# Seven Strassen products for the gate and up projections of an adaLN block

## The chip, the cores and the metric

The kernel runs on one core of a Trainium2 chip. Its engines are PE (TensorE, matmuls into PSUM), PEld (TensorE's weight loads, which overlap with PE), DVE (VectorE), ACT (ScalarE), POOL (GpSimd) and SP (SyncE, which issues the DMAs here). The metric is the device time of one execution in microseconds.

## The reference

One transformer block with adaptive layer norm on 2048 tokens of width 576: attention over the last 512 cached keys, then a gated feed-forward layer with 4608 hidden units. Everything is float32. Cut to what matters:

```python
h = _layernorm(x, axis=-1) * (1 + ca) + sa
x = x + ga * _A_ref(h, A_k_cache, A_v_cache, A_wq, A_wo)   # 32 heads of 128, 512 keys each
h = _layernorm(x, axis=-1) * (1 + cb) + sb
g = h @ w_gate                 # (2048, 576) x (576, 4608)
u = h @ w_up
x = x + gb * ((_sigmoid(g) * u) @ w_down)
```

The six rows sa, ca, ga, sb, cb, gb come from silu(c) @ w_mod.

## The kernel before, in words

Every matmul runs in `float32r`. To keep float32's accuracy, each operand is split into a high part (ACT copies it to `float32r`) and a low part (DVE or POOL subtracts the high part), and a product is three matmuls: high x low, low x high, high x high (`three`, `pairs_a`). The width 576 is four chunks of 128 and a tail of 64; the tail's high and low parts are laid on top of each other in 128 rows, so that it takes two matmuls. One product of 128 hidden units with a block of 512 tokens is so 14 matmuls of 512 columns.

Tokens are in four blocks of 512 (`blk`). Attention runs in two halves of two blocks each, 32 heads, written as a list of steps (`at_step`, `at_n`) in which weights, keys, norms and transposes of later steps are given a place by hand; a scheduler then fixes the order on each engine. The norms of the feed-forward layer for blocks 0 and 1 are at the end of this list (`norm_block(..., True, ...)`: DVE, POOL, five PE transposes per 128 tokens, ACT and DVE to write the two parts `hTm` and `hTt`). Blocks 2 and 3 follow in the first steps of the feed-forward loop.

The feed-forward loop goes over slices of 128 hidden units (`f`, 36 of them), and for each over the four blocks: 144 steps. A step computes gate and up for one block (L613: 28 matmuls of 512 columns into the banks `st` and `ot`), takes the sigmoid on ACT (L617), multiplies on DVE (L618), splits the result into `hs` (ACT L620, POOL L621), and beside it does the down products of the step two before: 8 tiles of three matmuls of 288 columns (L238, called from `down_mm`), each added into the residual `x` by DVE (L602). The weights of slice f+1 are loaded by SP (`load_a` L196 and L198, `load_b` L221) and split (ACT L203, POOL L204 and L205 for gate and up; POOL L225, ACT L227, POOL L229 for down) during slice f; each slice is loaded once for all four blocks. The pool of raw weights has four buffers, that of split weights four and two.

Around the loop, the last attention steps and the first feed-forward steps overlap, since the pools are shared and the first two slices are loaded from the attention's list of steps.

Of the kernel before, what the change touches and what calls it, by code (L numbers as in the profile page):

```python
# [16 lines left out]
P = 128  # L17
# [7 lines left out]
def adaln_block_kernel(ctx: ExitStack, tc: tile.TileContext, x, k_cache, v_cache, wq, wo, w_gate, w_up, w_down,  # L25
# [23 lines left out]
    wp = ctx.enter_context(tc.tile_pool(name="wp", bufs=1))  # L49
    ps = ctx.enter_context(tc.tile_pool(name="ps", bufs=1, space=bass.MemoryType.PSUM))  # L50
# [10 lines left out]
    def ps_qp():  # L61
        return psum("qp", 1, [P, BLK])
# [35 lines left out]
    ones = const.tile([P, P], F32, name="ones")  # L98
# [5 lines left out]
    def mod_rows(tag):  # L104
        return const.tile([P, D], F32, tag=tag, name=tag)
# [38 lines left out]
    def ln_stats(b, t):  # L144
        if t == 0:
            LN[b] = [wp.tile([P, TPB, 2], F32, tag="mv", name="mv", bufs=2),
                     wp.tile([P, TPB], F32, tag="ln_y", name="ln_y", bufs=2)]
        mv = LN[b][0]
        st = wp.tile([P, 2, 6], F32, tag="st", name="st", bufs=2)
        for j in range(2):  # L150
            nc.vector.bn_stats(st[:, j, :], xs[b][:, t, j * D2 : (j + 1) * D2])  # L151
        nc.vector.bn_aggr(mv[:, t, :], st)

    def ln_rsqrt(b):
        mv, y = LN[b]
        v = wp.tile([P, TPB], F32, tag="ln_v", name="ln_v", bufs=2)
        a = wp.tile([P, TPB], F32, tag="ln_a", name="ln_a", bufs=2)
# [88 lines left out]
    hTs = {}  # L246
    at = ctx.enter_context(tc.tile_pool(name="at", bufs=1))

    def new_hT(b, late):
        if late and b >= HB:  # L250
            main = at.tile([P, 2 * NC, BLK], F32R, tag="ptt", name="hTm2", bufs=2)
            tail = at.tile([P, 2, BLK], F32R, tag="vs", name="hTt2", bufs=2)
        else:
            main = wp.tile([P, 2 * NC, BLK], F32R, tag="hTm", name="hTm", bufs=2)
            tail = wp.tile([P, 2, BLK], F32R, tag="hTt", name="hTt", bufs=2)
        hTs[b] = (main, tail)

    load_x(0)
    scale, shift, gate = mod_rows("scale"), mod_rows("shift"), mod_rows("gate")
# [19 lines left out]
    new_hT(0, False)  # L279
# [9 lines left out]
    # order of the steps: both token blocks of a head in turn; at the ends of a half, where norms have to be  # L289
    # fitted in, both heads of a block in turn  # L290
# [111 lines left out]
    FA, FB, GA, GB = {}, {}, {}, {}  # L402
# [8 lines left out]
    # weights, keys and values that later steps need  # L411
# [23 lines left out]

    def load_f(f):
        FA[f] = [load_a(w_gate, f * P), load_a(w_up, f * P)]

    def split_f(f):
        GA[f] = [split_a(r) for r in FA.pop(f)]  # L440

    def load_d(f):
        FB[f] = load_b(w_down, f * P)

    def split_d(f):
        GB[f] = split_b(FB.pop(f), rows2["gate"])
# [47 lines left out]
    def norm_block(b, n_stats, n_apply, n_t, step, late, sc_, sh_, mul, add):  # L494
        for t in range(TPB):
            at_n(n_stats + t, ln_stats, b, t)
            at_n(n_apply + t * step, apply_late if late else ln_apply, b, t, sc_, sh_, mul, add)
            at_n(n_t + t * step, ln_transpose, b, t)
        at_n(n_stats + TPB, ln_rsqrt, b)
        at_n(n_t - 1, new_hT, b, late)  # L500

    def apply_late(b, t, scale_, shift_, *eng):
        ln_apply(b, t, rows2["scale"], rows2["shift"], *eng)

    n1 = N // 2
    norm_block(1, -12, -3, -2, 1, False, scale, shift, nc.vector, nc.vector)
    norm_block(2, n1 - 35, n1 - 20, n1 - 14, 2, False, scale, shift, nc.gpsimd, nc.gpsimd)
    norm_block(3, n1 - 30, n1 - 8, n1 - 6, 2, False, scale, shift, nc.gpsimd, nc.gpsimd)

    def mod_make2(key, m, j, add):  # L510
        if j == 0:
            rows2[key] = mod_rows(key + "2")
        mod_make(rows2[key], m, j, add)
# [7 lines left out]
    norm_block(0, N - 40, N - 20, N - 14, 2, True, None, None, nc.gpsimd, nc.gpsimd)  # L521
    norm_block(1, N - 35, N - 8, N - 6, 2, True, None, None, nc.gpsimd, nc.gpsimd)
    at_n(N - 13, load_f, 0)
    at_n(N - 8, split_f, 0)
    at_n(N - 5, load_f, 1)
    at_n(N - 6, load_d, 0)
    at_n(N - 3, split_f, 1)
    at_n(N, split_d, 0)
    at_n(N, load_d, 1)
    at_n(N + 4, split_d, 1)  # L530

# [20 lines left out]
    HS = {}  # L552
    LAG = 2
    order = [(f, b) for bs in ((0, 1), (2, 3)) for f in range(2) for b in bs]
    order += [(f, b) for f in range(2, NF) for b in range(NB)]
    M = len(order)
    turn = [0]

    def down_bank():
        turn[0] += 1  # L560
        return ps_qp()[:, :D2] if turn[0] % 3 == 0 else ps_wo()

    for b in range(HB, NB):
        new_hT(b, True)

    for m in range(0, M + LAG):
        if m < M:
            f, blk = order[m]
            if f > 0 and f + 1 < NF:
                if blk == 0 and f > 1 or f == 1 and blk == 2:  # L570
                    load_f(f + 1)
                if blk == 2 and f > 1 or f == 1 and blk == 3:
                    split_f(f + 1)
                    load_d(f + 1)
                if blk == 3:
                    split_d(f + 1)
        for b, m_stats, m_apply, m_t in ((2, 1, 2, 3), (3, 3, 3, 4)):
            for t in range(TPB):
                if m == m_stats:
                    ln_stats(b, t)  # L580
            if m == m_stats:
                ln_rsqrt(b)
            for t in range(TPB):
                if m == m_apply:
                    ln_apply(b, t, rows2["scale"], rows2["shift"], nc.vector, nc.gpsimd)
                if m == m_t:
                    ln_transpose(b, t)
        todo = []
        if 0 <= m - LAG < M:
            fd, bd = order[m - LAG]  # L590
            todo = [(fd, bd, t, j) for t in range(TPB) for j in range(2)]

        def down_some(k):
            for _ in range(k):
                if not todo:
                    return
                fd, bd, t, j = todo.pop(0)
                hs = HS[fd, bd]
                cols = slice(t * P, (t + 1) * P)
                p = down_mm(hs[:, 0, cols], hs[:, 1, cols], GB[fd], j, down_bank())  # L600
                xv = xs[bd][:, t, j * D2 : (j + 1) * D2]
                nc.vector.tensor_add(xv, p, xv)  # L602
                if fd == NF - 1 and j == 1:
                    nc.sync.dma_start(of[bd][:, t, :], xs[bd][:, t, :])

        if m < M:
            pg, pu = ps_sc(), ps_ot()
            gh = at.tile([P, 2, BLK], F32, tag="kt", name="gh", bufs=2)
            sg, hf = gh[:, 0, :], gh[:, 1, :]
            for p, sp in ((pg, GA[f][0]), (pu, GA[f][1])):  # L610
                pairs = pairs_a(sp, hTs[blk])
                for n, (l, r) in enumerate(pairs):
                    nc.tensor.matmul(p, l, r, start=n == 0, stop=n == len(pairs) - 1)  # L613
                    if n % 4 == 2:
                        down_some(1)
                if p is pg:
                    nc.scalar.activation(sg, pg, AF.Sigmoid)  # L617
            nc.vector.tensor_mul(hf, pu, sg)  # L618
            hs = at.tile([P, 2, BLK], F32R, tag="qt" if m % 2 else "ov", name="hs", bufs=2)
            nc.scalar.activation(hs[:, 0, :], hf, AF.Copy)  # L620
            nc.gpsimd.tensor_sub(hs[:, 1, :], hf, f32(hs[:, 0, :]))  # L621
            HS[f, blk] = hs
        down_some(len(todo))


# [26 lines left out]
```

## Time and profile before

| | |
|---|---|
| median of 3 runs | 3247.59 us (3245.72 to 3248.06) |
| profiled execution: span | 3245.9 us |
| PE busy in the span | 3209.9 us (99%) |
| DVE, ACT, POOL busy | 63%, 37%, 26% |
| granted TensorE clock, mean | 0.998 |
| HBM read, written | 103.52 MB, 4.72 MB |
| first feed-forward matmul, last matmul's end | 1837.6 us, 3241.2 us |

The page gives busy times over the whole span, then 40 equal slices, then the chain of work that ended last. PE is busy in all but the first slices; the ratio of DVE and ACT changes at about 1840 us, where attention ends and feed-forward begins. A busy PE is not PE at its peak, as matmuls are pipelined; how fast they follow each other is read from a timeline.

### The profile page before, as it was taken

What the parts mean: (1) busy time and instruction counts of PE and PEld (TensorE: products, weight loads), DVE (VectorE), ACT (ScalarE), POOL (GpSimd) and SP (SyncE); (2) the same over time, 40 slices, a digit from 0 to 9 for tenths busy, and PEclk for the clock granted to TensorE, in tenths of its full rate; (3) what the DMA queues carried; (4) which work ended last, traced back from release to release, by engine and by line L of the source; (5) the groups of instructions that cost most, each with busy time, mean ns of one, the idle gap of its engine ahead of it and who ended that gap; (6) DMA issues with size and microseconds to landing.
All of it is one profiled execution on the core that took longest, in us unless ns stands there. A gap on an engine that the chain in (4) does not pass through costs nothing.

```text
span 3245.9 us, 45972 instructions
## 1 busy us (share of the span) xinstructions
PE 3209.9 (99%) x17848; PEld 2782.2 (86%) x17848; DVE 2059.6 (63%) x4092; ACT 1211.2 (37%) x2520; POOL 837.2 (26%) x726
## 2 busy tenths in 40 slices
PE   7999999999999999999999999999999999999999
PEld 6888888888888888888888888888888888888888
DVE  8777777777797777777777954444444444444444
ACT  5555555555554555555555421111111111111111
POOL 3322212111132212112121332333322222233321
PEclk9999999999999999999999999999999999999999
DMA  5111111111011111111010000011100000001101
GB/s 176 34 41 45 45 33 35 33 30 37 27 30 33 34 33 34 33 30 37 27 37 27 24 21 24 24 28 28 28 24 25 24 24 24 24 24 28 29 15 59
DMA packets 126747, 111.22 MB, mean 34 GB/s; under 512 B 10432, under 2 KB 101568, under 8 KB 126016
## 3 DMA queue, kind: packets, MB, share of 16 engines
q1 hardware_dynamic: 126528, 108.27, 11.4%
q8 instruction: 141, 2.31, 0.3%
q14 instruction: 78, 0.64, 0.1%
HBM read 103.52 MB, written 4.72 MB: 33 GB/s over the span
## 4 chain that ended last, share of the span: by engine, by line
PE 93%; DVE 3%; DMA 1%; ACT 1%; issue 1%; POOL 0%; SPq 0%; ACTq 0%; POOLq 0%
PE wo L238 21%; PE qp L238 16%; PE st L613 14%; PE ot L613 14%; PE ot L238 10%; PE st L238 10%; PE st L368 7%; DMA raw<-in_A_wq_dram 1%; DVE h L170 1%; PE st L316 0%; ACT pp L357 0%; DVE st L151 0%; DVE x L395 0%; PE st L185 0%; POOL wb L229 0%
## 5 line engine op out<-in xcount | busy, mean ns | idle before, releaser
L602 DVE TENSOR_TENSOR x<-wo,x 128x288 f32<-128x288 f32 x768 | 344.8, 455 | 481.9 <-PE wo L238 481.7
L238 PE MATMUL wo<-wb,ov 128*128 128x288 f32 x3072 | 615.4, 308 | 1.1 <-DVE ov L386 1.1
L371 ACT ACTIVATE ptt<-st 128x512 fp32r<-128x512 f32 x512 | 305.6, 597 | 654.1 <-PE st L368 654.1
L395 DVE SCALAR_TENSOR_TENSOR x<-wo,rs,x 128x288 f32<-128x288 f32 x1024 | 513.1, 512 | 49.9 <-PE wo L238 0.8
L238 PEld LDWEIGHTS wo<-wb,ov 128*128 128x128 f32 x3072 | 482.2, 189 | 49.2 <-DVE ov L386 1.6
L355 DVE TENSOR_REDUCE neg<-st 128x1 f32<-128x512 f32 x512 | 352.0, 687 | 255.2 <-PE st L238 252.7
L613 PE MATMUL st<-hTm,wa 128*128 128x512 f32 x1728 | 493.7, 394 | 0.0
L613 PE MATMUL ot<-hTm,wa 128*128 128x512 f32 x1728 | 489.8, 392 | 0.0
L238 PE MATMUL qp<-hTm,wa 128*128 128x512 f32 x1536 | 444.2, 398 | 3.2 <-DVE hTm L189 1.8
L238 PE MATMUL ot<-ptt,vs 128*128 128x512 f32 x1536 | 442.7, 396 | 0.0
L238 PE MATMUL st<-kt,qt 128*128 128x512 f32 x1536 | 438.1, 393 | 0.1
L238 PEld LDWEIGHTS wo<-wb,hs 128*128 128x128 f32 x2304 | 380.5, 188 | 57.9 <-DVE x L602 3.2
L238 PE MATMUL wo<-wb,hs 128*128 128x288 f32 x2304 | 421.5, 295 | 2.1 <-DVE x L602 2.1
L621 POOL TENSOR_TENSOR hs<-gh,hs 128x512 fp32r<-128x512 f32 x144 | 186.7, 1296 | 749.4 <-ACT hs L620 746.8
L357 ACT ACTIVATE pp<-st,neg 128x512 f32<-128x512 f32 x512 | 350.5, 685 | 60.1 <-DVE neg L355 53.7
L372 DVE TENSOR_TENSOR ptt<-st,ptt 128x512 fp32r<-128x512 f32 x512 | 348.4, 680 | 33.2 <-ACT ptt L371 33.1
L613 PEld LDWEIGHTS ot<-hTm,wa 128*128 128x128 f32 x1728 | 308.7, 188 | 43.8
L204 POOL TENSOR_TENSOR wa<-raw,wa 128x512 fp32r<-128x512 f32 x136 | 176.7, 1299 | 647.1 <-ACT wa L203 572.2
L238 PEld LDWEIGHTS st<-kt,qt 128*128 128x128 f32 x1536 | 288.1, 188 | 62.6 <-DVE hTm L189 0.3
L613 PEld LDWEIGHTS st<-hTm,wa 128*128 128x128 f32 x1728 | 300.2, 187 | 33.3
L602 DVE TENSOR_TENSOR x<-qp,x 128x288 f32<-128x288 f32 x384 | 174.6, 455 | 239.8 <-PE qp L238 239.7
L368 PEld LDWEIGHTS st<-ident,pp 128*128 128x128 f32 x2048 | 253.2, 140 | 83.0 <-ACT pp L357 15.6
(86 smaller groups left out, 3416.8 us busy)
## 6 DMA issues: line engine op xcount, KB each, us to landing
raw<-in_A_wo_dram SPq DMA_DIRECT2D x64, 288.0 KB, 3.0
raw<-in_A_wq_dram SPq DMA_DIRECT2D x64, 256.0 KB, 3.0
raw<-in_B_w_down_dram SPq DMA_DIRECT2D x36, 288.0 KB, 2.8
raw<-in_B_w_gate_dram SPq DMA_DIRECT2D x36, 256.0 KB, 3.0
raw<-in_B_w_up_dram SPq DMA_DIRECT2D x36, 256.0 KB, 2.9
raw<-in_A_k_cache_dram SPq DMA_DIRECT2D x32, 256.0 KB, 2.7
raw<-in_A_v_cache_dram SPq DMA_DIRECT2D x32, 256.0 KB, 2.6
x<-in_A_x_dram SPq DMA_DIRECT2D x4, 1152.0 KB, 7.2
```

The source lines that it names most:

```text
L170: nc.vector.tensor_scalar(h, xs[b][:, t, :], mv[:, t, 0:1], y[:, t : t + 1], op0=OP.subtract, op1=OP.mult)
L204: nc.gpsimd.tensor_sub(sp[:, NC + 1 :, :], raw[:, :NC, :], f32(sp[:, :NC, :]))
L238: nc.tensor.matmul(p, l, r, start=first and n == 0, stop=last and n == len(pairs) - 1)
L355: nc.vector.tensor_reduce(NEG[b][:, i : i + 1], p, axis=AX.X, op=OP.max, negate=True)
L357: nc.scalar.activation(PP[n], p, AF.Exp, bias=NEG[b][:, i : i + 1], accum_out=SUM[b][:, i : i + 1])
L368: nc.tensor.transpose(p[:, k * P : (k + 1) * P], PP[n][:, k * P : (k + 1) * P], ident)
L371: nc.scalar.activation(PT[b][:, 0, :, cols], pv_, AF.Copy)
L372: nc.vector.tensor_sub(PT[b][:, 1, :, cols], pv_, f32(PT[b][:, 0, :, cols]))
L395: nc.vector.scalar_tensor_tensor(xv, p, RS[b][:, i : i + 1], xv, op0=OP.mult, op1=OP.add)
L602: nc.vector.tensor_add(xv, p, xv)
L613: nc.tensor.matmul(p, l, r, start=n == 0, stop=n == len(pairs) - 1)
L621: nc.gpsimd.tensor_sub(hs[:, 1, :], hf, f32(hs[:, 0, :]))
```

## The change

Gate and up of two token blocks are computed together. With the contraction of 576 cut into halves of 288, they are a product of two 2 x 2 matrices of blocks: A11 and A12 are the halves of a slice of `w_gate`, A21 and A22 those of `w_up`; B11 and B21 are the halves of the first block's normed tokens, B12 and B22 those of the second's. Strassen's scheme (in Winograd's form) makes the four results of seven products instead of eight, with sums of weights S1 to S4 and of tokens T1 to T4. A half is two chunks of 128 and a tail of 32; the tail is copied into four strips of 32 rows, which hold high or low parts so that one matmul covers all of the tail's part products. One product is seven matmuls of 512 columns.

- The blocks are taken as pairs (0, 1) and (2, 3), one after the other: 2 x 36 turns (`u`), each with seven products and 48 down matmuls. Each slice's weights are therefore loaded twice.
- The token operands, B11, B21, T1, T2, B22, T3, T4, are computed on DVE and POOL (`pair_norm`, `pair_sums`) and written to two tiles in DRAM, `scr`. For the first pair this is put into the second half of attention, for the second pair into turns 4 to 7. They are read back in two staging buffers (`stage`), transposed on PE and split (`load_combo`) before turn 0, and for the second pair in turn 35.
- The feed-forward has pools of its own, opened after attention's are closed, with `reuse_waits="tile"`. `rw` holds the raw weights of a turn and S1 to S4, with one buffer; `sw` the split ones, with two; `rd` the raw down weights, with one.
- Partial results are kept in SBUF by ACT (`keep`) or accumulated in the same PSUM bank (`a`, `b`, `c`), and added by DVE.

The core of the diff (line numbers of the new loop's functions run from 574 to 774):

```diff
+    def load_w(u):
+        f0 = (u % NF) * P
+        raw = fp.tile([P, 8, 3, P], F32, tag="rw", name="rw", bufs=1)
+        for w, parts in ((w_gate, (A11, A12)), (w_up, (A21, A22))):
+            for half, c in enumerate(parts):
+                r0 = half * D2
+                nc.sync.dma_start(raw[:, c, 0:2, :], w[r0 : r0 + 2 * P, f0 : f0 + P].rearrange("(s p) n -> p s n", p=P))
+                for q in range(4):
+                    nc.sync.dma_start(raw[q * TQ : (q + 1) * TQ, c, 2, :], w[r0 + 2 * P : r0 + D2, f0 : f0 + P])
+        RW[u] = raw
+
+    def sum_w(u):
+        r = RW[u]
+        nc.gpsimd.tensor_add(r[:, S1], r[:, A21], r[:, A22])
+        nc.gpsimd.tensor_sub(r[:, S2], r[:, S1], r[:, A11])
+        nc.gpsimd.tensor_sub(r[:, S3], r[:, A11], r[:, A21])
+        nc.gpsimd.tensor_sub(r[:, S4], r[:, A12], r[:, S2])
+
+    def split_w(u, a):
+        if u not in SW:
+            SW[u] = fp.tile([P, 7, 5, P], F32R, tag="sw", name="sw", bufs=2)
+        r, sw = RW[u][:, a], SW[u][:, a]
+        nc.scalar.activation(sw[:, 0:3, :], r, AF.Copy)
+        nc.vector.tensor_sub(sw[:, 3:5, :], r[:, 0:2, :], f32(sw[:, 0:2, :]))
+        up_ = slice(P // 2, P)
+        nc.gpsimd.tensor_sub(sw[up_, 2, :], r[up_, 2, :], f32(sw[up_, 2, :]))
...
+    def load_combo(pair, c):
+        t = STG.pop((pair, c))
+        ends = fp.tile([P, TPB, 4, TQ], F32, tag="ends", name="ends", bufs=1)
+        nc.scalar.activation(ends, t[:, :, None, 2 * P :].to_broadcast([P, TPB, 4, TQ]), AF.Copy)
+        hc = fp.tile([P, 5, BLK], F32R, tag="hc", name="hc", bufs=7)
+        HC[c] = hc
+        for s in range(3):
+            p = fpsum("w", 4, [P, BLK])
...
+            nc.scalar.activation(hc[:, s, :], p, AF.Copy)
+            if s < 2:
+                nc.vector.tensor_sub(hc[:, 3 + s, :], p, f32(hc[:, s, :]))
+            else:
+                for q in (1, 3):
+                    r = slice(q * TQ, (q + 1) * TQ)
+                    nc.vector.tensor_sub(hc[r, 2, :], p[r], f32(hc[r, 2, :]))
...
+    def product(u, a, c, p, first, downs=(2, 5)):
+        pairs = prod_pairs(u, a, c)
+        for n, (l, r) in enumerate(pairs):
+            nc.tensor.matmul(p, l, r, start=first and n == 0, stop=n == len(pairs) - 1, skip_group_check=not first)
+            if n in downs:
+                down_some(1)
+        if u + 1 < U:
+            split_w(u + 1, a)
...
+    for u in range(U + 1):
...
+        split_d(u)
+        if u + 1 < U:
+            sum_w(u + 1)
+            load_d(u + 1)
...
+        product(u, A11, B11, pa, True)
+        g0 = keep(pa, "g0")
+        product(u, A12, B21, pb, True)
+        nc.vector.tensor_add(g0, pb, g0)
+        nc.scalar.activation(g0, g0, AF.Sigmoid)
+        product(u, S1, T1, pc, True)
+        v1 = keep(pc, "v1")
+        product(u, S2, T2, pa, False)
+        g1 = keep(pa, "g1")
+        product(u, S4, B22, pc, False)
+        nc.vector.tensor_add(g1, pc, g1)
+        nc.scalar.activation(g1, g1, AF.Sigmoid)
+        product(u, S3, T3, pa, False, (2,))
+        nc.vector.tensor_add(v1, pa, v1)
+        nc.vector.tensor_mul(v1, v1, g1)
+        make_hs(u, 1, v1)
+        down_some(5)
+        product(u, A22, T4, pa, False, ())
+        nc.vector.tensor_mul(g0, pa, g0)
+        make_hs(u, 0, g0)
+        down_some(len(todo))
+        if u + 2 < U:
+            load_w(u + 2)
```

Left out above are the calls that stage and load the second pair's operands between the products of turn 35, and those of the second pair's norms (`late_tile`). `load_d` and `split_d` are as before but with one raw buffer; `make_hs` is ACT's copy and POOL's subtraction, as L620 and L621 were.

More of the change, by code (lines that the diff above doesn't have):

```diff
@@ L246, in adaln_block_kernel, with new_hT @@
     hTs = {}
[L247 to L255, printed above, removed]
+    at = actx.enter_context(tc.tile_pool(name="at", bufs=1))
+    def new_hT(b):
+        main = wp.tile([P, 2 * NC, BLK], F32R, tag="hTm", name="hTm", bufs=2)
+        tail = wp.tile([P, 2, BLK], F32R, tag="hTt", name="hTt", bufs=2)
         hTs[b] = (main, tail)
     load_x(0)
-    scale, shift, gate = mod_rows("scale"), mod_rows("shift"), mod_rows("gate")
+    scale, shift, gate = mod_rows("scale", wp), mod_rows("shift", wp), mod_rows("gate", wp)
     wm = {}
@@ new lines, in adaln_block_kernel, with pair_norm @@
+    norm_block(3, n1 - 30, n1 - 8, n1 - 6, 2, scale, shift, nc.gpsimd, nc.gpsimd)
+    scr = [dram.tile([7, P, TPB, D2], F32, tag=f"scr{i}", name=f"scr{i}") for i in range(2)]
+    def pair_norm(pair, t, h, eng):
+        for i in range(2):
+            b = 2 * pair + i
+            mv, y = LN[b]
+            nc.vector.tensor_scalar(h[i], xs[b][:, t, :], mv[:, t, 0:1], y[:, t : t + 1],
+                                    op0=OP.subtract, op1=OP.mult)
+            eng.tensor_mul(h[i], h[i], rows2["scale"])
+            eng.tensor_add(h[i], h[i], rows2["shift"])
@@ L549, in adaln_block_kernel @@
     assert not at_step
[L552 to L622, printed above, removed]
@@ new lines, in adaln_block_kernel, with fpsum, stage @@
+    actx.close()
+    fp = ctx.enter_context(tc.tile_pool(name="fp", bufs=1, reuse_waits="tile"))
+    fps = ctx.enter_context(tc.tile_pool(name="fps", bufs=1, space=bass.MemoryType.PSUM, reuse_waits="tile"))
+    def fpsum(tag, bufs, shape):
+        return fps.tile(shape, F32, tag=tag, name=tag, bufs=bufs)
+    TQ = P // 4
+    B11, B21, T1, T2, B22, T3, T4 = range(7)
+    A11, A12, A22, S1, S2, S3, S4, A21 = range(8)
+    HC, RW, SW, RD, SD, HS = {}, {}, {}, {}, {}, {}
+    STG = {}
+    def stage(pair, c):
+        t = fp.tile([P, TPB, D2], F32, tag="ts", name="ts", bufs=2)
+        nc.sync.dma_start(t, scr[pair][c])
+        STG[pair, c] = t
@@ new lines, in load_d, with split_d @@
+    def load_d(u):
+        f0 = (u % NF) * P
+        raw = fp.tile([P, D], F32, tag="rd", name="rd", bufs=1)
+        nc.sync.dma_start(raw, w_down[f0 : f0 + P, :])
+        RD[u] = raw
+    def split_d(u):
+        raw = RD.pop(u)
+        nc.gpsimd.tensor_mul(raw, raw, rows2["gate"])
+        sp = fp.tile([P, 2, D], F32R, tag="sd", name="sd", bufs=2)
+        nc.scalar.activation(sp[:, 0, :], raw, AF.Copy)
+        nc.gpsimd.tensor_sub(sp[:, 1, :], raw, f32(sp[:, 0, :]))
+        SD[u] = sp
```

168 lines of the change are left out of this document (129 added, 39 removed).

## The prediction

> **What bounds the kernel now.** I read the page from the top: busy times, then the chain of work that ended last. The share of PE (TensorE) in both is the first thing to see, since PE at 99% with a chain that is 93% PE leaves no other engine to relieve.
>
> ```profile
> span 3245.9 us, 45972 instructions
> PE 3209.9 (99%) x17848; PEld 2782.2 (86%) x17848; DVE 2059.6 (63%) x4092; ACT 1211.2 (37%) x2520; POOL 837.2 (26%) x726
> ...
> PE 93%; DVE 3%; DMA 1%; ACT 1%; issue 1%; POOL 0%; SPq 0%; ACTq 0%; POOLq 0%
> ```
>
> Shares over the span mix attention and feed-forward, so I asked for a stretch that holds feed-forward alone, and for the chain in order of time there. The stretch shows PE never idle at a granted clock of 1.00, DVE at 43%, POOL (GpSimd) at 30%. The chain rows give the pace: one gate/up/down step of one block each 3225.87 - 3216.24 = 9.63 us.
>
> ```profile
> 2100.00:3000.00 900.00, 900.00 (x4859) 787.79 (x4858) 388.54 (x840) 161.29 (x258) 267.92 (x233) 1.00 0.09 26
> ...
> 3216.24 0.93 PE st L613 x4
> 3225.87 0.93 PE st L613 x4
> ```
>
> What one matmul costs in a stream is not its duration, since matmuls overlap; the timeline of PE gives it from start to start.
>
> ```profile
> 2508.95 1.09 PE L613 MATMUL ot<-hTm,wa 128*128 128x512 f32 x4
> ...
> 2510.27 0.39 PE L613 MATMUL ot<-hTm,wa 128*128 128x512 f32 x1
> ...
> 2510.96 0.96 PE L238 MATMUL wo<-wb,hs 128*128 128x288 f32 x6
> ...
> L238 PE MATMUL wo<-wb,hs 128*128 128x288 f32 x2304 | 421.5, 295 | 2.1 <-DVE x L602 2.1
> L602 DVE TENSOR_TENSOR x<-wo,x 128x288 f32<-128x288 f32 x768 | 344.8, 455 | 481.9 <-PE wo L238 481.7
> ```
>
> (1.09 - 0.39) / 3 = 0.233 us for 512 columns, (0.96 - 0.30) / 5 = 0.132 us for 288. A step has 28 of the first and 24 of the second: 9.69 us, 0.6% over the 9.63 seen. So the step is its matmuls and nothing else.
>
> **Matmuls removed.** Two steps (two blocks, one slice of 128 hidden units) become one turn of the new loop: seven products of seven matmuls, 49 instead of 56, and the same 48 down matmuls. 49 x 0.233 + 48 x 0.132 = 17.75, scaled by 9.63/9.69 to 17.65 us, against 19.27. Over 72 turns that is 116 us off PE. ACT has under 9 us of work in a turn and DVE about 13 (16 x 0.455, five adds and products at 0.69, seven subtractions of 256 columns at 0.33), by the rows further down; if only work counted, PE would still set the pace.
>
> **The weight tile: a circle of waits.** The raw weights and their four sums lie in one tile, `rw`, with one buffer. In the built program the first load for turn u+2 waits until ACT, DVE and POOL have all finished splitting the seven combinations of turn u+1. Then twenty DMAs follow each other on SP's queue (four of 128 partitions, sixteen of 32; the old loop issues six for the four steps of a slice). Only after the twentieth can POOL add S1, then S2, then S4. The last split stands behind these on POOL, and the next load behind that. Nothing in the circle overlaps with itself, so its length is the pace of the loop if it is above 17.65 us.
>
> SP's part, from its timeline (64-partition strips are the nearest to the 32-partition ones) and from the DMA issues of the page:
>
> ```profile
> 10.82 1.19 SPq L198 DMA_DIRECT2D raw<-in_A_wq_dram  x2
> ...
> 2423.27 0.37 SPq L196 DMA_DIRECT2D raw<-in_B_w_up_dram  x1
> 2423.69 1.15 SPq L198 DMA_DIRECT2D raw<-in_B_w_up_dram  x2
> ...
> raw<-in_B_w_gate_dram SPq DMA_DIRECT2D x36, 256.0 KB, 3.0
> raw<-in_B_w_gate_dram SPq DMA_DIRECT2D x72, 32.0 KB, 2.6
> ```
>
> A wide issue takes 0.42 us to the next start, a strip 1.15 / 2 = 0.575. The last of the twenty starts 4 x 0.42 + 15 x 0.575 = 10.3 us after the first and lands 2.6 later: 12.9 us. Low end: every issue at 0.375, 9.7 us, but S3 and one `hs` subtraction stand ahead of S1 on POOL, so 10.3. High end: a 32-partition strip may cost more than a 64-partition one by as much as that costs more than a wide one (0.2 us): 16.
>
> POOL's part, from the costliest groups, with the timeline for the gap between two of its instructions and for the hop from another engine:
>
> ```profile
> L204 POOL TENSOR_TENSOR wa<-raw,wa 128x512 fp32r<-128x512 f32 x136 | 176.7, 1299 | 647.1 <-ACT wa L203 572.2 <-issue 74.9
> L229 POOL TENSOR_TENSOR wb<-raw,wb 128x576 fp32r<-128x576 f32 x100 | 143.2, 1432 | 652.5 <-ACT wb L227 652.4
> L205 POOL TENSOR_TENSOR wa<-raw,wa 64x128 fp32r<-64x128 f32 x136 | 62.7, 461 | 10.6
> L126 POOL TENSOR_TENSOR wm<-wm 128x288 f32<-128x288 f32 x24 | 19.5, 811 | 41.2 <-ACT wm L123 30.4 <-PE st L368 9.7 <-POOL wa L205 0.3
> ...
> 2498.48 1.29 POOL L204 TENSOR_TENSOR wa<-raw,wa 128x512 fp32r<-128x512 f32 x1 [2.40 <-ACT wa L203]
> 2499.85 0.46 POOL L205 TENSOR_TENSOR wa<-raw,wa 64x128 fp32r<-64x128 f32 x1
> ...
> 2501.52 0.74 ACT L203 ACTIVATE wa<-raw 128x640 fp32r<-128x640 f32 x1 [3.12 <-PE ot L613]
> 2502.39 1.30 POOL L204 TENSOR_TENSOR wa<-raw,wa 128x512 fp32r<-128x512 f32 x1 [2.08 <-issue]
> ```
>
> Sums are 384 wide: between 811 and 1299 ns by width, 1.02 us. In nearly all turns the program's order on POOL from S1 to the next load is S1, down-weight low part, S2, S4, two strips, `hs` low part, three strips, gate product, two strips: 3 x 1.02 + 2 x 1.43 + 1.30 + 7 x 0.46 = 10.45 us, and 13 gaps of 0.08: 11.5. Three hops at 2502.39 - 2502.26 = 0.13 add 0.4. Circle: 12.9 + 11.5 + 0.4 = 24.8 us.
>
> **DVE and POOL get in each other's way.** Seven of DVE's new subtractions per turn read two tiles of SBUF (weights and their high part). The old feed-forward loop has none of these in steady state, only such as read one tile in PSUM. Where they occur, beside POOL, at the start of feed-forward:
>
> ```profile
> L171 DVE TENSOR_TENSOR h<-h,scale x16: 739/746/1600, 15.0 to 1879.4; 128x576 f32<-128x576 f32 x16
> ...
> 1877.05 3.36 POOL L172 TENSOR_TENSOR h<-h,shift 128x576 f32<-128x576 f32 x2 [1.15 <-DVE h L171]
> 1881.20 1.43 POOL L172 TENSOR_TENSOR h<-h,shift 128x576 f32<-128x576 f32 x1 [0.79 <-DVE h L171]
> ...
> 1879.43 1.60 DVE L171 TENSOR_TENSOR h<-h,scale 128x576 f32<-128x576 f32 x1
> ```
>
> The instruction that takes 746 ns took 1600 beside POOL, and POOL's two took 3.36 where two alone take 2.94: POOL lost 0.42. Five of the seven fall inside POOL's part; each is 746 x 256 / 576 = 0.33 us. Between nothing and 5 x 0.33 = 1.65 I take half, 0.8, as the 0.42 is about half of the 0.75: the turn becomes 25.6 us. The Trainium skill (SBUF — State Buffer, "Who interferes with whom") states that a VectorE instruction with two SBUF inputs and a GpSimd one that reads SBUF take turns on a shared port, the second to issue blocked in full. The trace agrees for DVE's 1600 ns; by that rule POOL could lose all 1.65 us, and the turn would be 26.4 us, the kernel 55 us longer than my sum.
>
> PE's 17.65 us lie inside this: its turn waits at S2, whose bank is freed by an ACT copy that stands behind the split of S4, and it idles some 8 us there.
>
> **Edits that cost nothing.** Norms and sums of the first pair move into attention's second half: 4 x (4 x 1.43 + 4 x 0.81) = 36 us of POOL, which is mostly idle there (digits 12 to 22 of its 40 slices below), and eight DVE products, at most 8 x 1.6 = 13 us if that cover were gone. The stores of `scr` have their readers hundreds of us later.
>
> ```profile
> POOL 3322212111132212112121332333322222233321
> ```
>
> **Start, swap, end.** When does attention end without feed-forward products and late norms among it? The first row below is a stretch with L613's matmuls alone, the others are timeline, stretch and groups.
>
> ```profile
> 1836.00:1846.00 10.00, 5.45 (x18) 3.10 (x19) 1.00 0.10 30
> ...
> 1845.08 0.56 PE L238 MATMUL wo<-wb,ov 128*128 128x288 f32 x3
> ...
> 1846.00:1905.00 59.00, 53.64 (x289) 44.72 (x288) 49.03 (x108) 15.06 (x37) 23.23 (x17) 1.00 0.03 9
> ...
> L185 PE MATMUL st<-ident,h 128*128 128x128 f32 x128 | 19.6, 279 | 9.7 <-DVE h L172 9.1 <-DVE hTm L189 0.6
> L186 PE MATMUL wo<-ident,hd 128*128 128x128 f32 x32 | 9.5, 297 | 1.4 <-ACT hd L179 1.4
> ...
> 3240.65 0.56 PE L238 MATMUL qp<-wb,hs 128*128 128x288 f32 x3
> ```
>
> 1845.6 less 18 feed-forward matmuls (4.2) and the transposes of eight token tiles (at most a quarter of 19.6 and of 9.5): 1835. From there to the start of the fourth load I take 70 us, an estimate: the first load is hidden behind attention, the second waits for DVE's statistics of blocks 2 and 3 (14), then come a short turn (19) and one (37) with staging transfers of `hc` among its loads and the second pair's sums on POOL. Bounds: 45 if only two short turns show, 95 if three full turns and a swap's ACT work do. The swap at u = 35 puts 7 x (0.64 + 3 x 0.60) = 17 us on ACT and as much on DVE; some 15 us longer, but the program's order in the five turns after it puts strips ahead of S1, 3 to 4 us shorter each: 0, give or take 15. After the last load 25.6 us to its last split, then PE's rest of turn 70 from S2 on (6), turn 71 (17.65), 48 matmuls (6.3) and the 5 us that follow the last matmul now (3240.65 + 0.56 to 3245.9): 61 in all.
>
> ```profile
> L617 ACT ACTIVATE gh<-st 128x512 f32<-128x512 f32 x144 | 86.0, 597 | 526.4 <-PE st L613 526.4
> L618 DVE TENSOR_TENSOR gh<-ot,gh 128x512 f32<-128x512 f32 x144 | 99.6, 692 | 42.2 <-PE ot L613 40.9 <-PE wo L238 0.6 <-PE qp L238 0.6
> L620 ACT ACTIVATE hs<-gh 128x512 fp32r<-128x512 f32 x144 | 91.8, 638 | 508.0 <-DVE gh L618 506.1
> ```
>
> Sum: 1835 + 70 + 68 x 25.6 (fourth load to last) + 61 = 3707 us of span. The profiled span of 3245.9 lies 1.7 under the median of the three runs, 3247.59, so **3709 us**, 14% slower.
>
> **Rivals.** *PE sets the pace after all.* If the loads and sums of a turn were done by the time PE wants them, the change pays: 3247.6 - 116, plus some 39 for a first turn in which PE has no down matmuls and waits for seven staged operands (50 us against its 11), plus 15 for the swap, less the 5 us that PE idles now from 1846 to 1905: 3181. It decides below a circle of 17.65 us, 8 less than mine; all twenty issues at 0.375, no lock and no gaps still leave over 21. Speaks for it: two thirds of my circle are bounded by rows of other shapes. Chance 0.04.
> *Cheap issues.* Strips issue like wide loads and the lock is free: 10.3 + 11.5 + 0.4 = 22.2 us, 68 x 3.4 less: 3478. The wide issue's 0.37 speaks for it, the strips' 0.575 against. Chance 0.15.
> *Dear strips, full lock.* 16.0 + 11.5 + 0.4 + 1.65 would be 29.5; half of the strips' excess gives 28: 3872. Chance 0.15.
> *The change doesn't do what it says.* The built program has 3528 = 72 x 49 gate/up matmuls and unchanged 6528 of 288 columns, so this would have to be an equality by accident; 0.01.
>
> **How the numbers follow.** My forecast holds the remaining 0.65, at 25.6 us a turn. The range takes in cheap issues with a start of 45 (3450) and dear strips with a start of 95 (3900). Faster and slower are meant beyond 0.2%, about what the runs' spread of 2.3 us lets one tell: faster 0.04, same 0.01, slower 0.95.
>
> **What would show it.** In the changed profile: a PE pause of 6 to 10 us ahead of the S2 product in each turn and PE at 65 to 75% in feed-forward, with a granted clock under 1.00 behind the pauses; SP issuing strips 0.5 to 0.6 us apart and stopping until POOL's last strip; POOL back to back from S1 to that strip; load to load 25 to 26 us; the chain running through DMA and POOL. Wrong if load to load is set by PE products, if the twenty issues take under 8 us, or if turns differ widely from each other.

## The result and the profile after

The changed kernel takes 3539.11 us (median, 3536.31 to 3542.53), against 3246.65 us for the kernel before on the same chip: 1.090 times as long, 95% interval 1.0884 to 1.0915. The prediction was 3709 us, range 3450 to 3900.

The page of the changed kernel, in the order in which that of before was read (busy times, chain, the DMA issues of the weight tile with their count, size and us to landing):

```profile
span 3539.1 us, 50078 instructions
...
PE 3241.9 (92%) x17432; PEld 2745.2 (78%) x17432; DVE 2597.1 (73%) x4828; ACT 1548.7 (44%) x3212; POOL 1408.3 (40%) x1486
...
PE 51%; POOL 20%; SPq 14%; DMA 4%; issue 4%; DVE 3%; ACT 3%; POOLq 0%; ACTq 0%; DVEq 0%
...
rw<-in_B_w_gate_dram SPq DMA_DIRECT2D x144, 128.0 KB, 2.2
...
rw<-in_B_w_gate_dram SPq DMA_DIRECT2D x576, 16.0 KB, 1.8
```

PE has 416 instructions fewer and is busy for 92% of the span instead of 99%. The chain, 93% PE before, now runs through POOL, SP's queue and the DMAs for 38%. In a stretch of feed-forward alone, which holds the turn of the swap too (columns: PE, PEld, DVE, ACT, POOL busy, granted clock, DMA share), no engine is full any more, and the clock is below 1.00:

```profile
2200.00:2800.00 600.00, 512.59 (x2656) 426.20 (x2655) 428.16 (x770) 223.20 (x423) 344.39 (x392) 0.98 0.20 57
```

One turn on SP's queue and the start of the next, 23.30 us later, and what SP waited for in that stretch (us in total, times, longest):

```profile
2308.69 0.39 SPq L609 DMA_DIRECT2D rw<-in_B_w_gate_dram  x1
2309.12 1.85 SPq L611 DMA_DIRECT2D rw<-in_B_w_gate_dram  x4
2311.02 0.43 SPq L609 DMA_DIRECT2D rw<-in_B_w_gate_dram  x1
2311.49 3.04 SPq L611 DMA_DIRECT2D rw<-in_B_w_gate_dram  x4
...
2317.41 1.86 SPq L611 DMA_DIRECT2D rw<-in_B_w_up_dram  x4
...
2331.99 0.39 SPq L609 DMA_DIRECT2D rw<-in_B_w_gate_dram  x1
...
SPq L609 <- DVE sw L626: 179.4, 26, 7.4
...
SPq L609 <- POOL sw L628: 21.3, 25, 2.2
```

Four strips go out in 1.85 us, 0.46 each. From the first issue to the last it takes 8.98 us in the median turn (one group in some turns stalls, as the one of 3.04 us here; why is open). Before it starts the next round, SP stands (179.4 + 21.3) / 26 = 7.7 us for the splits of the turn before, first DVE's, then POOL's last strip. That is the circle of the prediction. Load to load, mean over the turns 46 to 68, POOL's instructions stand so (us after the first load; start + duration): S3 8.94 + 1.08, `hs` 10.16 + 1.32, S1 11.64 + 1.14, down low part 12.74 + 1.56, S2 14.25 + 1.20, S4 15.53 + 1.02, strips 16.63 and 17.12, `hs` 17.66 + 1.34, strips 19.07, 19.48, 19.90, gate product 20.45 + 1.49, strips 22.01 and 22.49 + 0.46. The next load starts at 22.98.

PE's timeline in such a turn (the bracket is idle time before the row, and what ended it):

```profile
2282.92 0.96 PE L674 MATMUL a<-hc,sw 128*128 128x512 f32 x3 [1.40 <-ACT g L682]
...
2285.89 0.67 PE L240 MATMUL w<-sd,hs 128*128 128x288 f32 x3 [0.91 <-DVE x L667]
...
2287.63 0.96 PE L674 MATMUL c<-hc,sw 128*128 128x512 f32 x3 [0.84 <-ACT v L682]
```

The longest pause, 1.40 us, is ahead of S2 and ends with ACT's copy `g`, as the prediction had it; but others follow at S4 and among the down products. From 2300 to 2600 us, steady turns alone, PE is idle for 48.2 of 300 us, 3.7 in a turn.

The end of attention is the other place. The same 10 us on four engines:

```profile
1007.28 0.79 POOL L506 TENSOR_TENSOR hs<-h 128x288 f32<-128x288 f32 x1
1008.03 0.79 POOL L508 TENSOR_TENSOR hs<-h 128x288 f32<-128x288 f32 x1
1008.78 0.79 POOL L507 TENSOR_TENSOR hs<-h,hs 128x288 f32<-128x288 f32 x1
1009.65 0.79 POOL L509 TENSOR_TENSOR hs<-h,hs 128x288 f32<-128x288 f32 x1
...
1010.47 0.58 DVE L499 TENSOR_SCALAR h<-x,mv,ln_y 128x576 f32<-128x576 f32 x1 [5.39 <-POOL hs L509]
...
1014.39 0.69 ACT L355 ACTIVATE pp<-st,neg 128x512 f32<-128x512 f32 x1 [5.85 <-DVE neg L353]
...
1012.23 1.35 PE L240 MATMUL wo<-wb,ov 128*128 128x288 f32 x3 [4.32 <-DVE x L393]
```

The scheduler had moved all four token tiles of the early norms to one place, 984 to 1023 us, though they are written 12 steps apart from step 312 on. Norms and sums share four buffers, so DVE's next product (L499) waits 5.39 us until POOL has finished the sums; attention's row maxima (L353) and residual additions (L393) queue behind it on DVE, and ACT and PE stand. This occurs three times (DVE's waits from 980 to 1020 us), and attention ends at 1849.8 us.

```profile
DVE h L499 <- POOL hs L509: 12.1, 3, 5.4
```

### The profile page after: what moved, and what is told of

It reads as the page before. It is cut to its first block, busy times and chain, and to the rows that moved or that the text cites. A ratio compares the mean times of both kernels' runs of the same rounds, so it can differ in the third digit from the quotient of the medians.

```text
span 3539.1 us, 50078 instructions
## 1 busy us (share of the span) xinstructions
PE 3241.9 (92%) x17432; PEld 2745.2 (78%) x17432; DVE 2597.1 (73%) x4828; ACT 1548.7 (44%) x3212; POOL 1408.3 (40%) x1486
## 4 chain that ended last, share of the span: by engine, by line
PE 51%; POOL 20%; SPq 14%; DMA 4%; issue 4%; DVE 3%; ACT 3%; POOLq 0%; ACTq 0%; DVEq 0%
PE qp L240 11%; SPq L611 11%; PE wo L240 11%; PE ot L240 9%; PE st L240 9%; PE st L366 6%; POOL sw L628 4%; DMA rw<-in_B_w_up_dram 3%; SPq L609 3%; POOL hs L688 3%; POOL sd L641 3%; POOL rd L638 2%; POOL rw L617 2%; POOL rw L616 2%; POOL rw L619 2%
## 5 line engine op out<-in xcount | busy, mean ns | idle before, releaser
L240 PEld LDWEIGHTS w<-sd,hs 128*128 128x128 f32 x3456 | 568.8, 196 | 222.9 <-DVE x L667 84.9
L240 PE MATMUL w<-sd,hs 128*128 128x288 f32 x3456 | 640.8, 307 | 106.8 <-DVE x L667 57.5
L674 PE MATMUL a<-hc,sw 128*128 128x512 f32 x2016 | 580.9, 405 | 86.7 <-ACT g L682 86.7
L626 DVE TENSOR_TENSOR sw<-rw,sw 128x256 fp32r<-128x256 f32 x504 | 454.6, 923 | 241.3 <-ACT sw L625 241.1
L667 DVE TENSOR_TENSOR x<-w,x 128x288 f32<-128x288 f32 x1152 | 482.1, 448 | 192.2 <-PE w L240 191.8
L393 DVE SCALAR_TENSOR_TENSOR x<-wo,rs,x 128x288 f32<-128x288 f32 x1024 | 513.5, 512 | 50.1 <-PE wo L240 0.5
L353 DVE TENSOR_REDUCE neg<-st 128x1 f32<-128x512 f32 x512 | 352.5, 688 | 260.9 <-PE st L240 257.9
L674 PEld LDWEIGHTS a<-hc,sw 128*128 128x128 f32 x2016 | 367.9, 193 | 158.0 <-ACT g L682 108.1
L625 ACT ACTIVATE sw<-rw 128x384 fp32r<-128x384 f32 x504 | 249.0, 521 | 327.4 <-POOL rw L617 133.6
L674 PE MATMUL c<-hc,sw 128*128 128x512 f32 x1008 | 334.9, 427 | 53.8 <-ACT v L682 52.5
L231 POOL TENSOR_TENSOR wb<-raw,wb 128x576 fp32r<-128x576 f32 x64 | 91.5, 1429 | 634.6 <-ACT wb L229 634.5
L366 PE MATMUL st<-ident,pp 128*128 128x128 f32 x2048 | 307.8, 273 | 5.9 <-ACT pp L355 5.1
```

The costliest lines, as they stand in the source:

```text
L240: nc.tensor.matmul(p, l, r, start=first and n == 0, stop=last and n == len(pairs) - 1)
L353: nc.vector.tensor_reduce(NEG[b][:, i : i + 1], p, axis=AX.X, op=OP.max, negate=True)
L366: nc.tensor.transpose(p[:, k * P : (k + 1) * P], PP[n][:, k * P : (k + 1) * P], ident)
L393: nc.vector.scalar_tensor_tensor(xv, p, RS[b][:, i : i + 1], xv, op0=OP.mult, op1=OP.add)
L625: nc.scalar.activation(sw[:, 0:3, :], r, AF.Copy)
L626: nc.vector.tensor_sub(sw[:, 3:5, :], r[:, 0:2, :], f32(sw[:, 0:2, :]))
```

## The experiments

All are the changed kernel with the edit shown; ratios are to the kernel before, run on the same chip.

**1. The circle opened** (two_raw). The raw weights get two buffers, the sums a tile of their own (three `hs` buffers instead of four make room).

```diff
-        raw = fp.tile([P, 8, 3, P], F32, tag="rw", name="rw", bufs=1)
+        raw = fp.tile([P, 4, 3, P], F32, tag="rw", name="rw", bufs=2)
...
+        s = fp.tile([P, 4, 3, P], F32, tag="su", name="su", bufs=1)
-        nc.gpsimd.tensor_add(r[:, S1], r[:, A21], r[:, A22])
+        nc.gpsimd.tensor_add(s[:, 0], r[:, 2], r[:, 3])
```

> The raw weights get two buffers of their own and the four sums a tile apart (hs has three buffers instead of four to make room), so the loads of a turn no longer wait for the splits of the turn before. Theory of the circle (issue, landing, POOL from S1 to the last strip): the circle is open, the turn falls from 22.9 us to PE's 17.65 or a little over, 18 to 19.5; with 68 turns the time is 3539 less 230 to 350, 3190 to 3310. Rival, DVE and POOL blocking each other set the pace: all of their work stays, the turn stays over 21.5, the time over 3440.

Measured: 3216.25 us, ratio 0.9907 (0.9892 to 0.9922), a little faster than before the change. The turn is 17.88 us. Two first issues of a turn, the same stretch and the chain inside a turn:

```profile
2503.08 0.39 SPq L612 DMA_DIRECT2D rw<-in_B_w_gate_dram  x1
...
2520.96 0.38 SPq L612 DMA_DIRECT2D rw<-in_B_w_gate_dram  x1
...
2200.00:2800.00 600.00, 598.23 (x3275) 519.13 (x3275) 505.46 (x947) 266.32 (x520) 438.21 (x493) 1.00 0.24 69
...
by line: PE w L240 35.8%; PE a L679 34.5%; PE c L679 22.0%; PE b L679 8.0%
```

In steady turns PE does not pause, the chain is PE alone, and the clock is at 1.00, with the same twenty issues (8.99 us from first to last in the median turn) and the same work on POOL and DVE. So no engine and no queue was too slow; the wait was the whole loss in the loop.

**2. Only the sums' tile** (own_sums). As 1, but the raw weights keep one buffer (`bufs=1`).

> One buffer for the raw weights as in the change, but S1 to S4 in a tile of their own, so that of the two edits of two_raw only the one is made. Circle of waits through the one buffer: the last reader of the raw weights is the split of A22, whose low part still stands last on POOL, so the next load begins where it did: turn 22.9 us, 3539, give or take 15. Rival (it was the sums in the raw tile that held the load back, not the single buffer): the load needs no longer wait for the splits of S1 to S4, turn under 19 us, 3300 or less.

Measured: 3542.25 us, ratio 1.091 (1.0893 to 1.0927); turn 23.0 us.

```profile
2200.00:2800.00 600.00, 516.08 (x2620) 428.47 (x2619) 424.41 (x759) 219.45 (x418) 342.47 (x390) 0.96 0.20 57
...
SPq L612 <- DVE sw L631: 172.9, 26, 7.4
```

SP waits as in the changed kernel. With one buffer for the raw weights it makes no difference where the sums lie; it is the second buffer that opens the circle. No run has two buffers with the sums left inside.

**3. Fewer issues in the circle** (half_strips). The strips of both K halves go in one transfer, 12 issues for 20.

```diff
-                for q in range(4):
-                    nc.sync.dma_start(raw[q * TQ : (q + 1) * TQ, c, 2, :], w[r0 + 2 * P : r0 + D2, f0 : f0 + P])
+            tails = w.rearrange("(c k) f -> k c f", c=2)[2 * P : D2, :, f0 : f0 + P]
+            for q in range(4):
+                nc.sync.dma_start(raw[q * TQ : (q + 1) * TQ, parts[0] : parts[0] + 2, 2, :], tails)
```

> One DMA takes the 32-row strips of both K halves of a weight matrix, so a turn issues 12 DMAs instead of 20; POOL's and DVE's work is unchanged. Circle: 8 issues of 0.464 us less, 3.7 us, less some 0.4 for a longer landing (32 KB against 16 KB): turn 19.6, time 3539 - 68 x 3.3 = 3315 (3285 to 3350). Rival, DVE and POOL blocking each other: nothing on them changes, time over 3500.

Measured: 3453.55 us, ratio 1.0639 (1.0623 to 1.0655); turn 21.6. The direction was right, the size a miss. The issues do take 3.7 us less (5.30), and S1 starts at 7.64 us instead of 11.64. POOL's timeline shows where 2.6 of these 4.0 us went:

```profile
2506.52 1.05 POOL L617 TENSOR_TENSOR rw<-rw 128x384 f32<-128x384 f32 x1 [7.21 <-DMA rw<-in_B_w_up_dram]
2507.53 1.01 POOL L619 TENSOR_TENSOR rw<-rw 128x384 f32<-128x384 f32 x1
2508.51 1.01 POOL L618 TENSOR_TENSOR rw<-rw 128x384 f32<-128x384 f32 x1
2509.60 1.06 POOL L620 TENSOR_TENSOR rw<-rw 128x384 f32<-128x384 f32 x1
2510.62 1.44 POOL L689 TENSOR_TENSOR hs<-v,hs 128x512 fp32r<-128x512 f32 x1
```

S1 (L617) waits for the landing, and S3 (L619, 1.18 in the mean of the turns 46 to 68) and one `hs` (L689, 1.42) now stand behind it. In the changed kernel both ran ahead of S1, while the last loads were under way. S3 cannot do so here, since it reads A21, whose strips now arrive with A22's at the very end. A shorter load so uncovers work that it had hidden.

**4. POOL relieved** (strips_dve). The low parts of the strips go to DVE.

```diff
-        nc.gpsimd.tensor_sub(sw[up_, 2, :], r[up_, 2, :], f32(sw[up_, 2, :]))
+        nc.vector.tensor_sub(sw[up_, 2, :], r[up_, 2, :], f32(sw[up_, 2, :]))
```

> The seven subtractions of the tail strips (64 partitions x 128) move from POOL to DVE. Circle: POOL's part loses seven instructions of 0.46 us and their gaps, 3.6 us; DVE gets 7 x 0.2 more, and the load waits for DVE's last one instead, so some of it is lost again: turn 19.5 to 21, time 3310 to 3410. Rival, blocking sets the pace: DVE has 14 instead of 7 instructions with two SBUF inputs in a turn, each waiting for POOL, time 3500 or more.

Measured: 3472.72 us, ratio 1.0697 (1.0681 to 1.0713); turn 22.0, above what was expected and short of the rival's 3500. The circle now closes on DVE, whose last strips stand among residual additions and a product. In the chain, the last four steps and the next load:

```profile
2520.47 0.33 DVE sw L626
2520.81 0.29 DVE sw L628
2521.13 0.46 DVE x L667
2521.59 0.03 issue
2521.62 0.30 DVE sw L628
2521.94 0.04 issue
2521.98 0.39 SPq L609
```

The seven strips take 5.1 us a turn on DVE (turns 46 to 68), where 1.4 were reckoned: 0.29 us each in the median, up to 1.44. In the chain from 2500 to 2524 us L626 has 19.1%, L628 11.8% and POOL nothing. So the rival has a part in this run: subtractions that DVE stretches beside POOL now lie on the circle; how much of the miss they make is not told apart. Work that leaves POOL shortens the circle only until another engine ends it.

**5. The lock taken away** (no_dve_sub). The low parts of the weights' wide chunks are not computed; ACT copies raw values there, so that DVE has no more two-input subtractions from SBUF beside POOL.

```diff
-        nc.vector.tensor_sub(sw[:, 3:5, :], r[:, 0:2, :], f32(sw[:, 0:2, :]))
+        nc.scalar.activation(sw[:, 3:5, :], r[:, 0:2, :], AF.Copy)
```

> The low parts of the weights' two 128-row chunks are not computed: ACT copies the raw weight into their place, DVE's seven subtractions with two SBUF inputs are gone. Circle: only what these take from POOL's instructions is won, 0.3 to 0.8 us a turn, and ACT's seven more copies of 0.4 us are not on the circle: time 3539 - 68 x 0.5 = 3505 (3480 to 3525). Rival, blocking sets the pace: DVE's subtractions last 0.92 us in the mean instead of 0.41, and with them gone the turn falls by 3 us or more: under 3340.

Measured: 3461.81 us, ratio 1.0664 (1.0646 to 1.0682); turn 21.88, 1.10 less than the changed kernel's: more than the 0.8 expected, far from the rival's 3. The groups on POOL in the stretch from 2200 to 2800 us (busy, mean ns), first of the changed kernel, then of this one:

```profile
L617 POOL TENSOR_TENSOR rw<-rw 128x384 f32<-128x384 f32 x26 | 30.7, 1180 | 0.2
L616 POOL TENSOR_TENSOR rw<-rw 128x384 f32<-128x384 f32 x26 | 28.9, 1112 | 10.2 <-DMA rw<-in_B_w_up_dram 9.3 <-issue 0.3
```

```profile
L617 POOL TENSOR_TENSOR rw<-rw 128x384 f32<-128x384 f32 x27 | 27.4, 1014 | 2.0
L616 POOL TENSOR_TENSOR rw<-rw 128x384 f32<-128x384 f32 x27 | 27.4, 1013 | 3.0 <-DMA rw<-in_B_w_up_dram 0.7 <-POOL sw L628 0.3
```

With DVE's subtractions gone, POOL's sums take the 1.01 us that the prediction had for their width. The Trainium skill (SBUF — State Buffer, "Who interferes with whom") lets the second to issue wait in full; here that was mostly DVE, whose subtraction (L626) takes 408 ns at the least and 1655 at the most:

```profile
L626 DVE TENSOR_TENSOR sw<-rw,sw x504: 408/784/1655, 1857.0 to 3499.0; 128x256 fp32r<-128x256 f32 x168
```

In the turns 46 to 68 DVE's seven take 6.74 us a turn, 3.9 more than 7 x 0.408, and of those that overlap with no POOL instruction none takes over 0.43. POOL loses less: the thirteen instructions listed from S1 on add up to 11.08 us in the changed kernel and the same thirteen to 10.44 here, so 0.64 of the 1.10 us is the lock itself; the rest came with another order on POOL and is not told apart.

**6. What a strip costs** (strips64). Two strips of 64 rows instead of four of 32, the tails then being other rows of the weights.

```diff
-                for q in range(4):
-                    nc.sync.dma_start(raw[q * TQ : (q + 1) * TQ, c, 2, :], w[r0 + 2 * P : r0 + D2, f0 : f0 + P])
+                for q in range(2):
+                    nc.sync.dma_start(raw[q * 64 : (q + 1) * 64, c, 2, :], w[r0 + 2 * P - 32 : r0 + D2, f0 : f0 + P])
```

> The four 32-row strips of a part are loaded as two of 64 rows (rows of the weights that don't belong there, so the tail products are of other numbers): 12 issues a turn instead of 20, 32 KB each instead of 16. It tells what mis-sized the issue. If a 64-row strip costs 0.575 us here too, as in the kernel before, and 32-row ones 0.464, the price goes by rows or size; then 8 x 0.575 + 4 x 0.44 and a landing of 2.6 make a turn of 20.5, time 3375. If it costs 0.464 here as well, it was the place and not the strip: turn 19.6, time 3315.

Measured, one run: 3467.57 us; turn 21.8.

```profile
2505.20 0.37 SPq L609 DMA_DIRECT2D rw<-in_B_w_gate_dram  x1
2505.62 1.11 SPq L611 DMA_DIRECT2D rw<-in_B_w_gate_dram  x2
2506.77 0.59 SPq L609 DMA_DIRECT2D rw<-in_B_w_gate_dram  x1
```

1.11 / 2 = 0.56 us for a strip of 64 rows, against 1.85 / 4 = 0.46 for one of 32, on the same queue. The 0.575 that the prediction took is that of 64 rows. Issue by issue (medians of the turns 46 to 68) the price goes by what stands ahead, and hardly by the transfer itself: behind a 32-row strip 0.42 us, be it a strip or a wide load that follows; behind a 64-row strip 0.59 for a wide load and 0.60 for a strip; behind a wide load 0.46 to 0.48 for either. Size doesn't show: behind the 32 KB strips of experiment 3, which have 32 rows too, it is 0.43.

The turn missed the 20.5 expected by 1.3. S1 starts at 8.89, which is the sum of the issues and the landing as expected; but one `hs` (1.42) that had run ahead of S1 now stands behind S4, as in experiment 3.

**7. Attention: DVE's products moved to POOL** (early_pool). First theory for the end of attention: DVE stands in its queue, so the eight first products of the early norms go to POOL.

```diff
-            nc.vector.tensor_scalar(h[i], xs[b][:, t, :], mv[:, t, 0:1], y[:, t : t + 1],
-                                    op0=OP.subtract, op1=OP.mult)
+            (nc.gpsimd if pair == 0 else nc.vector).tensor_scalar(
+                h[i], xs[b][:, t, :], mv[:, t, 0:1], y[:, t : t + 1], op0=OP.subtract, op1=OP.mult)
```

> The first operation of the first pair's norms in attention (x minus mean, times the inverse deviation) moves from DVE to POOL; the rest is unchanged. Theory: attention lost 11 us at 985 to 1016 us because DVE, in order, waited up to 5.4 us for a buffer that POOL's sums held, with the softmax's row maxima queued behind it; without that wait the 11 us come back: 3528. Rival: POOL's burst of norm and sums itself delays the weights that attention needs next, then POOL's longer burst keeps or adds to the loss: 3539 to 3550.

Measured: 3551.13 us, ratio 1.094 (1.0925 to 1.0955); attention ends at 1858.0, 8 us later still. The theory in this form fell.

```profile
993.40 2.29 POOL L499 TENSOR_SCALAR h<-x,mv,ln_y 128x576 f32<-128x576 f32 x1
...
1039.06 0.74 ACT L205 ACTIVATE wa<-raw 128x640 fp32r<-128x640 f32 x1 [22.78 <-DMA raw<-in_A_wq_dram]
```

DVE no longer waits, but the product takes 2.29 us on POOL instead of 0.58, the bundle is longer, and the splits of attention's weights behind it on POOL come late. ACT stands 22.78 us for the next query weights: their load starts at 1035.80, when POOL's split at 1034.37, behind the bundle, has freed a buffer. SP's queue, too, holds fifteen stores of the bundle's results ahead of this load, each waiting for POOL, the last until 1034.44. The bundle itself, not DVE's queue alone, had to go.

**8. Attention without the early norms** (no_early). On 1, with the residual stored in their place.

```diff
-        pair_norm(0, t, PH[t], nc.gpsimd)
...
-        pair_sums(0, t, PH.pop(t), ta, tb, nc.gpsimd)
+        for c in (0, 2, 4):
+            nc.sync.dma_start(d[:, c : c + 2, t, :], xs[0][:, t, :].rearrange("p (c d) -> p c d", c=2))
```

> two_raw with the norms and sums of the first pair left out of attention: the residual itself is stored as token operands, so the feed-forward layer of the first pair works on other numbers, with the same instructions. If the bundle of these norms on POOL at 985 to 1016 us is what moved the end of attention by 11 to 14 us: last attention matmul at 1835 to 1839, 3202 to 3206. Rival (attention is longer for another reason, the pools that are split in two or the missing overlap with feed-forward): attention ends where it did, 3213 to 3217.

**9. The same norms, kept apart** (pinned). On 1; all the work is done, but DVE's first products keep their written places.

```diff
-            nc.vector.tensor_scalar(h[i], xs[b][:, t, :], mv[:, t, 0:1], y[:, t : t + 1],
-                                    op0=OP.subtract, op1=OP.mult)
+            k = nc.vector.tensor_scalar(h[i], xs[b][:, t, :], mv[:, t, 0:1], y[:, t : t + 1],
+                                        op0=OP.subtract, op1=OP.mult)
+            if pair == 0:
+                tc.keep_in_program_order(k)
```

> two_raw with one word more: the eight DVE products that begin the early norms keep their written place among the other instructions of attention, 12 steps from one token tile to the next, so that POOL gets them apart instead of in one bundle. If the bundle costs the 11 us and not the work: no POOL instruction of the weights waits behind more than one tile's 9 us, 3203 to 3208. Rival (the work itself costs it, wherever it stands): 3213 to 3217.

Measured: no_early 3201.88 us (ratio 0.9867, 0.9852 to 0.9882), pinned 3202.54 (0.9868, 0.9853 to 0.9882). Attention ends at 1832.5 and 1834.7 us, against 1847.7 in experiment 1. The stretch that held the bundle, in the changed kernel and in pinned:

```profile
984.00:1016.00 32.00, 22.70 (x105) 18.30 (x105) 18.63 (x35) 9.62 (x21) 26.43 (x24) 0.89 0.29 98
```

```profile
984.00:1016.00 32.00, 32.00 (x185) 27.70 (x184) 24.01 (x45) 15.36 (x34) 2.69 (x2) 1.00 0.05 12
```

PE has 105 matmuls in the first and 185 in the second, POOL 26.43 us of work and 2.69. In pinned one token tile of norms and sums takes POOL some 9 us, and then it is free for the weights:

```profile
1178.96 3.09 POOL L503 TENSOR_TENSOR h<-h,scale 128x576 f32<-128x576 f32 x2 [0.39 <-DVE h L499]
...
1187.33 0.81 POOL L511 TENSOR_TENSOR hs<-h,hs 128x288 f32<-128x288 f32 x1
1192.73 1.31 POOL L206 TENSOR_TENSOR wa<-raw,wa 128x512 fp32r<-128x512 f32 x1 [4.59 <-ACT wa L205]
```

Spread, the norms cost within 1 us of what leaving them out costs. The order was the loss. Attention's end also moves by itself: in the changed kernel and experiments 1 to 6, whose attention is written alike, it lies between 1847.4 and 1849.8.

**10. The best version** (pinned_half). Experiments 9 and 3 together.

> pinned, with the strips of both K halves in one transfer, 12 for 20 a turn. With two buffers SP's queue is off the path, so by the circle theory this is worth nothing in a steady turn and at most the 2 to 5 us that the first turns and the turn of the swap wait for loads: 3200 to 3208, within 5 us of pinned. Rival (the queue of issues still sets part of the turn's 17.88 us against 17.65 of matmuls): 0.1 to 0.2 us a turn, 7 to 15 us less than pinned.

Measured: 3196.77 us, ratio 0.9851 (0.9835 to 0.9867), 49 us faster than before; 5.8 less than pinned, a little over what was expected. The turn stays at 17.89 us (17.90 in pinned), so the rival fell. Attention ends 2.3 us sooner, within the scatter of that place, and PE's pauses from 1838 to 1890 us add up to 16.3 us instead of 18.2, of which one in pinned and the one at its place here are

```profile
1860.10 1.11 PE L599 MATMUL w<-ident,ends 128*128 128x128 f32 x4 [5.49 <-ACT ends L592]
```

```profile
1859.05 0.63 PE L599 MATMUL w<-ident,ts 128*128 128x128 f32 x4 [1.10 <-DVE hc L602]
```

The cause of the other 1.6 us is open.

## Why the prediction was right, and where it was off

The step that decided it held: a single buffer, refilled over SP's queue only after the last split and read only after the last load, sets the pace instead of PE. Experiment 1 opens it and all of the loss goes; experiment 2 shows that it is the buffer. The number owes something to luck: the forecast was 170 us too high, the turns alone 179, and the 15 us that attention lost, which it had at nothing, hid a part of that. The range was wide because it was to hold cheap issues too. The sums, in us:

| term | predicted | measured |
|---|---|---|
| end of attention | 1835 | 1849.8 |
| to the start of the fourth load | 70 | 66.5 |
| 68 turns | 68 x 25.6 = 1741 | 68 x 22.98 = 1562.3 |
| after the last load | 61 | 60.4 |
| span | 3707 | 3539.1 |

- **Issue of a strip** (mis-sized). 0.575 was that of 64 partitions; 32 take 0.46. The direction of the doubt was wrong too: the high end supposed that fewer rows cost more. And the price is that of the transfer ahead (experiment 6).
- **Landing** (mis-sized): 1.8 us for 16 KB instead of 2.6 for 32 KB. It is not the size: 32 KB land in 1.8 to 1.9 us in experiment 3 and in 2.1 in 6. With the issues, the twentieth lands at 8.98 + 1.8 = 10.8 us in the median turn, not at 12.9.
- **Ahead of S1** (missing from the forecast, named only at its low end). At 10.8, POOL is still in the `hs` subtraction that began at 10.16, and S1 starts at 11.64. In 6 of 22 turns a stalled issue or a late landing still makes it wait, 0.2 to 1.2 us. So only 1.3 us of the 2.1 won came through, and experiment 3 lost more in the same way.
- **POOL's part**: 22.95 - 11.64 = 11.3 us against 11.5 and 0.8 for the lock. The work and the order were as listed. The lock is 0.64, but the gaps of 0.08 between instructions are nearly absent in a stream: durations add up to 11.08 of 11.3. Nor do the hops of 0.4 show: the next load starts 0.03 after the last strip. DVE's subtraction takes 0.41 alone, not 0.33.
- **The turn**, 22.98, lies nearer to the rival of cheap issues (22.2, 3478 us) than to 25.6; that rival had a chance of 0.15. Its free lock was wrong, and its 10.3 us to S1, which did count S3 and `hs`, was 1.3 short.
- **Edits that cost nothing** failed. The cover was looked for in POOL's idle share over slices of 80 us, but where on POOL the scheduler would put the work was not read. The price given for a lost cover, 13 us, is by luck the 13.0 between attention's ends in experiments 1 and 9 (15.1 from 1 to 8): it is not DVE's slower products but its queue behind a buffer.
- **PE's pauses** were too large in the forecast, and in one place. A turn is 23.0 - 17.9 = 5.1 us longer than PE needs, where 8 were forecast. 3.7 of it are pauses, the longest 1.40 in the rows above, where 6 to 10 at once were to be seen; the other 1.4 lie in matmuls that take longer. So PE is busy for 85% in the row above, not 65 to 75%, though its work is 17.9 / 22.98 = 78% of a turn. The clock fell to 0.98 as said, and to 0.95 from 2850 to 3300 us.
- **Swap**: the turn of the swap takes 36.4 us, 13.4 more than a steady one (15 forecast), and the four after it 21.9, 17.9, 18.6 and 20.6, which gives 12.9 back (forecast: all of it).
- **PE sets the pace after all**: its condition was not met, but its price is now tested. 3181 was forecast; pinned, with the circle open and attention clean, takes 3202.5. The turn is 17.9 instead of 17.65, 72 x 0.25 = 18 us (why PE needs 0.25 more is open); the other terms were good to 4 together.

## What to carry to other kernels

Ask of every buffer what must happen between its last reader and its next first reader; if load, sums and splits of one buffer follow each other, their sum is the pace, however idle each engine looks, and shortening one link won less here than a second buffer did, since other work moved into the gap. Price an issue by a row that stands behind the same kind of transfer. A moved piece of work is hidden only where the built order puts it: read that order for bundles and for the buffers that they share.

## What the runs showed of the hardware

- How long an issue takes on SP's queue goes by the transfer ahead of it: 0.42 us behind a strip of 32 partitions, 0.46 to 0.48 behind a wide load of 128, 0.59 to 0.60 behind a strip of 64, for wide loads and strips alike (the changed kernel, half_strips, strips64). Why is open.
- Where DVE and POOL both read SBUF, DVE loses more: its 256-column subtraction ranges from 0.41 to 1.65 us, while POOL's 384-column sums go from 1.01 to 1.18 in the mean. A turn of 23 us with seven such subtractions costs DVE 3.9 us and POOL 0.64.
- A product with a scalar per partition takes 2.29 us on POOL and 0.58 on DVE for 576 columns, 3.9 times as long; a product of two tiles of that width takes POOL only 1.42 (L501, early_pool). The Trainium skill (GPSIMD Engine Reference, "4.1 Engine selection") calls GpSimd roughly line-rate with one input; the rows here differ, and the rows decide.
